# Attention with sorted key blocks, then a token mixer: turning q by head pairs laid side by side on GpSimd

## The chip, the cores and the metric

The kernel runs on one core of a Trainium2 chip. A core has five engines that run their own queues in order and wait for each other through semaphores: TensorE (PE in the profile: matmuls and transposes into PSUM), VectorE (DVE), ScalarE (ACT), GpSimd (POOL) and SyncE (SP, which here only issues transfers). The metric is the device time of one execution in microseconds. The kernel before takes 104.41 us (median of 3 runs, 104.3 to 104.9). The profile shows one execution; its span of 102.3 us leaves out some microseconds at the ends of the device time.

## What is computed

The reference, cut to what matters, with B = 4 batches, H = 8 heads, S = 768 tokens, D = 64, and 8 blocks of 96 tokens:

```python
P = sort_net                                   # (B, H, 8, 8), five rounds of row and column softmax
k_sorted = einsum('bhij,bhjcd->bhicd', P, k_blocks)
v_sorted = einsum('bhij,bhjcd->bhicd', P, v_blocks)
attn = softmax(q_block @ k_sorted_block.T / sqrt(D))      # inside each block of 96
x    = concat_heads(attn @ v_sorted_block)                # (B, S, 512)
W    = (x @ w_q) @ (x @ w_k).T / sqrt(64)                 # token mixer, (S, S) per batch
out  = relu(W @ x) @ w_out                                # (B, S, 512), float32
```

The inputs q, k and v are float32, each 1.5 MB a batch, and become bf16 as they are loaded.

## The kernel before

The kernel is written as a list of units. The text `ORDER` is that list: each item has a letter for its kind, the batch, a number, and at its end an engine (A, D, P or S) or, for TensorE units, a PSUM bank. A loop at the end of the kernel emits the items as they stand, so this order is the order on each engine's own queue; what one engine must wait for from another follows from the data. Nothing reorders at run time. A capital letter is TensorE work, and the small letter of the same name moves its result out of PSUM on ScalarE or VectorE.

For one batch the stages are these. `l` loads an input in the GpSimd queue (`l20P` is q of batch 2; the middle digit is the batch, the last 0 for q, 1 for k, 2 for v, 3 and 4 for weights). Tokens lie on partitions: token 6p + r is on partition p at position r. `n` builds the sorting matrices M from the 8x8 matrices, on GpSimd for batches 1 to 3. `Q` transposes q, `q` copies it to QT. `K` multiplies k by M, which sorts and transposes it, and `k` copies it to KT. `V` (or `F` and `A` for batch 0) sorts v; `R` moves the sorted rows between partitions by transfers of the SP queue. `S` and `e` give the scores and their exponentials, `P`, `r` and `x` the attention result, `T` and `t` its transpose. `J`, `W`, `G` and `H` are the token mixer, `d` copies a half of its query part to other partitions (on ScalarE, on VectorE, or by a transfer), `O`, `o` and `y` give and store the output. `Z` is fill: matmuls of zeros that keep TensorE running at the start, while the 8x8 softmax rounds (`c`) go on. `N` copies a single element on GpSimd out of a tile that is still being made: it holds the GpSimd queue, and so the loads behind it, back until that tile is there. The batches overlap: while batch 1 has its scores computed, batch 0 is in the mixer.

Around the change. A `Q` unit covers two of the six positions r and all four head pairs, so there are three units a batch. Each unit has 16 transposes (lines 244 to 250): one head at a time, 128 tokens by 64 dimensions as the stationary operand, the identity as the moving one with 128 columns. The two heads of a pair go to the lower and the upper half of the PSUM partitions. Its result fills one bank, which `q` copies out at once (line 252). The tiles Qn, Kn and Vn have three buffers each (lines 95 and 96), chosen by the batch modulo 3. The first half of q of batch 0 is loaded as float32 by SP into a borrowed tile, and ScalarE casts it into Qn (items `i04A`, `i05A`, lines 185 to 187); the second half comes by `l00P`.

The transposes, the copies out and all matmuls are recorded under the helper lines 140 (`mm`) and 144 or 146 (`copy`), so the profile's groups are told apart by the tiles.

Of the kernel before, what the change touches and what calls it, by code (L numbers as in the profile page):

```python
# [9 lines left out]
BF16 = mybir.dt.bfloat16  # L10
# [5 lines left out]


ORDER = """
l00P l01P l02P i00P i02P l03P c00D c01D i01D Z080 l11P c02D i03A Z250 c03D Z350 i04A l10P c04D Z440
i05A Q027 c05D Q016 q02A Q005 Z540 q00A b00D l12P B004 Z020 q01A n01D n00D l04P K010 u00A n03D K002  # L20
n11P n02D k01A K036 k00D K024 k03A S020 n10P k02D S012 e02A S056 F034 e01A S000 f03D l20P e05A F022
A035 f02A S066 a03D e00A A024 F012 e06A a02D F000 f01A K136 n21P f00D P044 A013 r04D A002 k13D a01A
n20P K100 x04D S036 k10A a00D K114 e03A S040 k11D P002 e04A P016 r00D Q115 x00D r01D P020 x01D q11A
Q104 r02D P032 q10A x02D V116 T005 v11A N11v l21P l30P r03D Q124 x03D V100 t00A V126 q12A v10D T015
T033 T022 v12A N11v N10v N12v l22P t03D S110 l32P t02D t01A S123 V136 e11A J012 v13D J005 e12A J032
S150 R12S j01D J025 R15S e15A S106 j00D R10S Q214 R11S d01D l31P Q203 e10A R14S q21D R13S W002 Q225
q20D d00A S160 w00D W014 q22A K126 w01D G003 e16A n30P k12A G013 K230 g01D K224 n31P k23A S136 k22D
H002 e13A K200 h00D S244 k20A H026 h02A S200 K212 e20A k21D O057 e24A H010 o05D S212 O046 h01A S234
e21A O007 e23A O033 o00D o04A P140 S264 o03A y02S Q302 r14D e26A x14D P116 S144 r11D Q313 x11D e14A
P100 q30A P134 r10D x10D V206 q31A O022 r13D x13D v20A V230 T103 v23A P126 T135 t10A r12D V210 x12D  # L30
O014 o02A v21A y01S V222 t13D T117 o01D v22A T126 V330 t11D y00S V304 t12D R20S S252 v30A Q327 R21S
v33D R25S J106 e25A R24S q32D R22S J115 R23S J126 V310 j10A J135 S222 v31D j11A W104 V326 e22A d11S
W115 w10D K300 v32D d10A G104 k30A K322 R30S K336 R32S w11A S300 k32A R33S k33D G114 R31S e30A R35S
K312 g11D R34S S366 k31D S354 e36A H110 e35A H106 h11D S312 h10A S334 P210 e33A O107 r21D e31A x21D
P204 O116 o10A r20D x20D P230 o11A P222 r23D H124 y10S x23D T207 h12A O126 r22D x22D t20A P300 O145
o12A r30D x30D T214 o14A T227 P242 t21D S325 t22A S340 r24D O134 x24D e32A T237 e34A o13D P312 J205
t23A y11S r31D P330 x31D J214 J225 P326 r33D j20A x33D J234 T303 d20S j21A W202 O155 t30A r32D d21S
w20D x32D W212 G203 w21A o15D P340 T312 r34D G213 y12S x34D T327 t31D g21A T336 t32D H220 t33A H202
H214 h22D J307 J316 h21D J327 O251 j30A d30A W300 h20D J336 O247 w30A j31A o25D G300 d31A o24A W316
O221 y22S w31D G310 o22A O237 g31A H320 o23A H312 H304 h32A O206 y21S O217 o20A O351 o21A h30D h31A  # L40
O340 y20S o35A O307 o34D y38S O321 y37S o30A O310 y33S o32D O337 o31A y35S y34S o33B y36S
"""


# [1 line left out]
def kernel(  # L46
# [11 lines left out]
    nc = tc.nc  # L58
    B, H, S, D = q.shape
# [3 lines left out]
    P = 128  # L63
    R6 = S // P
    SP = BLK // R6
    NP = H // 2
# [16 lines left out]
    sb = ctx.enter_context(tc.tile_pool(name="sb", bufs=1))  # L83
    psp = ctx.enter_context(tc.tile_pool(name="psp", bufs=1, space=bass.MemoryType.PSUM))

    def tiles(name, n, shape, dtype=BF16):
        return [sb.tile(shape, dtype, name=f"{name}{i}") for i in range(n)]

    PS = psp.tile([P, 8, 512], FP32, name="ps")
    ENG = {"A": nc.scalar, "D": nc.vector, "P": nc.gpsimd, "S": nc.sync}  # L90
# [2 lines left out]
    nc.sync.dma_start(out=Pm[:, 0:NB, :], in_=sort_net.rearrange("b h i j -> (b h) i j"))  # L93

    NIN = 3
    Qn, Kn, Vn = (tiles(n, NIN, [P, H, R6, D]) for n in ("Qn", "Kn", "Vn"))
    wqk = sb.tile([P, PT, 2, DH], BF16, name="wqk")
    wo = sb.tile([P, PT, DM], BF16, name="wo")

    def load(t, src, b):  # L100
        nc.gpsimd.dma_start(out=t[b % NIN].rearrange("p h r d -> p h (r d)"),  # L101
                            in_=src[b].rearrange("h (p r) d -> p h (r d)", p=P))

    QT = tiles("QT", 2, [P, NP, R6, P])
# [20 lines left out]
    idb = sb.tile([P, P], BF16, name="idb")  # L125
# [13 lines left out]
    def mm(o, w, x, start=True, stop=True, t=False):  # L139
        nc.tensor.matmul(o, w, x, is_transpose=t, start=start, stop=stop, skip_group_check=True)  # L140

    def copy(e, o, i):
        if e == "A":
            nc.scalar.copy(o, i)  # L144
        else:
            nc.vector.tensor_copy(o, i)  # L146

    def bf(n):
        return PS[:, n, :].bitcast(BF16)
# [3 lines left out]
    stage = mixT[0].rearrange("p a c r s -> p (a c r s)").bitcast(FP32).rearrange("p (h e) -> p h e", h=HQ)  # L153
# [21 lines left out]
    def u_i(b, n, e):  # L175
        if n == 0:
            nc.gpsimd.memset(idb, 0.0)
            nc.gpsimd.affine_select(out=idb, in_=idb, compare_op=ALU.not_equal, fill=1.0, base=0,
                                    pattern=[[-1, P]], channel_multiplier=1)
        elif n == 1:  # L180
            nc.vector.reduce_max(m_p, idb.rearrange("p (j s) -> p s j", s=SP), axis=AX.X)
        elif n == 3:
            nc.scalar.copy(Lx.rearrange("p i j s -> p (i j) s"),
                           idb[0:BH, 0:BH].unsqueeze(2).to_broadcast([BH, BH, SP]))
        elif n in (4, 5):
            h = 2 * n - 8
            copy(e, Qn[0][:, h:h + 2].rearrange("p h r d -> p h (r d)"), stage[:, h:h + 2])
        elif n == 2:
            for t in VT:
                nc.gpsimd.memset(t.rearrange("p i (h e) -> p i h e", e=DS)[:, :, :, D:DS], 1.0)  # L190
            for t in Vs:
                nc.gpsimd.memset(t[:, :, :, D:DS], 1.0)
            for t in KT:
                nc.gpsimd.memset(t[:, :, S:S + P - BLK], 0.0)
            for t in E:
                nc.gpsimd.memset(t[:, :, 2 * TH * BLK:EW], 0.0)
                nc.gpsimd.memset(t[:, NT - 1, 2 * (NB * NP - TH * (NT - 1)) * BLK:EW], 0.0)  # L197


    def u_l(b, n, e):  # L200
        if n == 3:
            for s, w in enumerate((moe_w_q, moe_w_k)):
                nc.gpsimd.dma_start(out=wqk[:, :, s, :], in_=w.rearrange("(t p) d -> p t d", p=P))  # L203
        elif n == 4:
            nc.gpsimd.dma_start(out=wo, in_=moe_w_out.rearrange("(t p) d -> p t d", p=P))
        elif b == 0 and n == 0:
            nc.gpsimd.dma_start(out=Qn[0][:, HQ:H].rearrange("p h r d -> p h (r d)"),  # L207
                                in_=q[0, HQ:H].rearrange("h (p r) d -> p h (r d)", p=P))
        else:
            load((Qn, Kn, Vn)[n], (q, k, v)[n], b)  # L210
# [30 lines left out]
            mm(PS[:, bank, :], filw[:, b, :], fil)  # L241


    def u_Q(b, n, bank):
        ps = bf(bank).rearrange("p (k r s) -> p k r s", k=NP, r=2)
        for r in range(2):
            for kp in range(NP):
                for hh in range(2):
                    mm(ps[hh * D:(hh + 1) * D, kp, r, :], Qn[b % NIN][:, 2 * kp + hh, 2 * n + r, :],
                       idb, t=True)  # L250

    def u_q(b, n, e, bank):
        copy(e, QT[b % 2][:, :, 2 * n:2 * n + 2, :].rearrange("p k r s -> p k (r s)"),
# [225 lines left out]
    for item in ORDER.split():  # L479
        kind, b, n, arg = item[0], int(item[1]), int(item[2:-1]), item[-1]  # L480
# [40 lines left out]
```

## Time and profile before

| what | before |
|---|---|
| device time, median of 3 | 104.41 us |
| span of the profiled execution | 102.3 us |
| granted TensorE clock | 1.00 on the mean |
| transposes of q | 192 in 12 units |
| GpSimd M for batches 1 to 3 | 6, 1.30 us each |
| loads issued by GpSimd | 15, 0.76 to 0.95 us of GpSimd each |
| QT copies | 9 on ScalarE at 1.02 us, 3 on VectorE at 0.68 us |

The page has one row for each group of instructions: line, engine, operation, result and operands, count, then busy time and mean duration, then the idle time of the engine just before. Durations of matmuls are latencies and overlap; the time that a unit takes is read from the start of its first matmul to the start of the next unit's. The part of the page in slices shows the rest: TensorE's row stands at 8 or 9 tenths from the start to the end, and the transfer row at 9 from the second slice to the 26th, some 2.5 to 66 us; after that transfers are few. GpSimd is busy in the first 40 us and idle afterwards.

```profile
PE   3999988889879998899999999789999999999940
POOL 5999667550018954000000000000000000000000
DMA  1899999999999999999999999641305150234992
```

### The profile page before, as it was taken

What the parts mean: (1) busy time and instruction counts of PE and PEld (TensorE: products, weight loads), DVE (VectorE), ACT (ScalarE), POOL (GpSimd) and SP (SyncE); (2) the same over time, 40 slices, a digit from 0 to 9 for tenths busy, and PEclk for the clock granted to TensorE, in tenths of its full rate; (3) what the DMA queues carried; (4) which work ended last, traced back from release to release, by engine and by line L of the source; (5) the groups of instructions that cost most, each with busy time, mean ns of one, the idle gap of its engine ahead of it and who ended that gap; (6) DMA issues with size and microseconds to landing.
All of it is one profiled execution on the core that took longest, in us unless ns stands there. A gap on an engine that the chain in (4) does not pass through costs nothing.

```text
span 102.3 us, 3324 instructions
## 1 busy us (share of the span) xinstructions
PE 91.3 (89%) x1411; PEld 59.3 (58%) x1420; DVE 71.2 (70%) x135; ACT 76.4 (75%) x115; POOL 24.6 (24%) x41
## 2 busy tenths in 40 slices
PE   3999988889879998899999999789999999999940
PEld 1234566678657686545867668556778665544410
DVE  3776787589987874653898966779979999304420
ACT  5254979949859997999699789995896446678430
POOL 5999667550018954000000000000000000000000
PEclk9999999999999999999999999999999999999999
DMA  1899999999999999999999999641305150234992
GB/s 17 280 212 205 202 193 199 203 208 201 204 208 204 207 200 247 254 217 204 209 297 205 317 352 202 172 132 77 135 0 210 40 205 0 87 136 195 372 345 103
DMA packets 19133, 19.57 MB, mean 191 GB/s; under 512 B 1904, under 2 KB 17200, under 8 KB 19120
## 3 DMA queue, kind: packets, MB, share of 16 engines
q0 software_dynamic: 13552, 9.70, 62.3%
q1 hardware_dynamic: 5568, 9.67, 28.1%
q8 instruction: 11, 0.18, 0.7%
q14 instruction: 2, 0.02, 0.0%
HBM read 20.19 MB, written 6.29 MB: 259 GB/s over the span
## 4 chain that ended last, share of the span: by engine, by line
PE 47%; DMA 30%; POOL 9%; ACT 7%; issue 2%; DVE 2%; ACTq 0%; DVEq 0%; POOLq 0%
PE ps L140 47%; DMA Vn<-in_v_dram 18%; DMA Kn<-in_k_dram 9%; DMA qD<-qkT 3%; POOL Kn L101 2%; ACT E L347 2%; ACT KT L144 1%; POOL wqk L203 1%; DVE mixT L453 1%; POOL E L197 1%; ACT qkT L144 1%; ACT mixT L451 1%; POOL Qn L207 1%; POOL Vn L101 1%; POOL Qn L101 1%
## 5 line engine op out<-in xcount | busy, mean ns | idle before, releaser
L347 ACT ACTIVATE E<-ps 96x960 bf16<-96x960 f32 (+1 forms) x28 | 24.0, 913 | 0.9 <-PE ps L140 0.9
L140 PE MATMUL ps<-wo,mixT 128*128 128x512 bf16 x88 | 22.5, 380 | 0.5
L381 DVE TENSOR_TENSOR X<-ps,R 96x896 bf16<-96x896 f32 (+1 forms) x20 | 20.1, 1006 | 0.6
L140 PEld LDWEIGHTS <-mixT 128*128 128x128 bf16 x96 | 8.5, 98 | 9.3 <-issue 0.8
L144 ACT COPY ot<-ps 128x512 f32<-128x512 f32 (+1 forms) x16 | 9.2, 581 | 5.2 <-PE ps L140 5.2
L140 PE MATMUL ps<-VT,E 96*128 96x65 bf16 x256 | 11.0, 193 | 0.7 <-DVE mixT L453 0.7
L140 PEld LDWEIGHTS <-E 96*128 96x128 bf16 x256 | 9.7, 97 | 2.9 <-issue 0.9
L140 PE MATMUL ps<-fil,filw 128*128 128x512 bf16 x27 | 9.3, 500 | 2.0 <-DVE filw L161 1.6
L453 DVE TENSOR_SCALAR mixT<-ps 128x1024 bf16<-128x1024 f32 x6 | 7.2, 1220 | 5.0 <-PE ps L140 4.9
L146 DVE COPY ot<-ps 128x512 f32<-128x512 f32 (+1 forms) x9 | 5.9, 658 | 6.0 <-PE ps L140 4.6
L140 PE MATMUL ps<-QT,KT 64*128 64x96 bf16 x256 | 9.8, 204 | 0.3 <-ACT KT L144 0.3
L144 ACT COPY QT<-ps 128x1024 bf16<-128x1024 bf16 x9 | 8.8, 1016 | 0.7 <-PE ps L140 0.6
L146 DVE CAST KT<-ps 128x768 bf16<-128x768 f32 x8 | 7.5, 948 | 2.5 <-PE ps L140 2.5
L231 POOL TENSOR_TENSOR M<-PTR,m_p 128x512 bf16<-128x512 bf16 x6 | 7.8, 1314 | 4.9 <-PE ps L140 3.1
L140 PEld LDWEIGHTS <-KT 64*128 64x128 bf16 x256 | 6.6, 94 | 3.9 <-issue 1.5
L140 PE MATMUL ps<-M,Kn 128*64 128x128 bf16 x192 | 7.6, 221 | 1.3 <-ACT XT L144 0.5
L140 PEld LDWEIGHTS <-Kn 128*64 128x64 bf16 x192 | 6.1, 109 | 3.1 <-DMA Kn<-in_k_dram 1.2
L140 PEld LDWEIGHTS <-X 96*128 96x128 bf16 x128 | 6.4, 98 | 1.6 <-issue 0.4
L140 PE MATMUL ps<-idb,X 96*128 96x96 bf16 x128 | 7.3, 206 | 0.0
L144 ACT CAST KT<-ps 128x768 bf16<-128x768 f32 x8 | 6.4, 799 | 0.9 <-PE ps L140 0.9
L140 PE MATMUL ps<-idb,Qn 128*64 128x128 bf16 x192 | 7.1, 221 | 0.0
L140 PEld LDWEIGHTS <-filw 128*128 128x128 bf16 x28 | 2.9, 118 | 7.1 <-issue 2.7
(77 smaller groups left out, 137.8 us busy)
## 6 DMA issues: line engine op xcount, KB each, us to landing
out_dram<-ot SPq DMA_DIRECT2D x9, 512.0 KB, 3.5
Kn<-in_k_dram POOLq DMA_DIRECT2D x4, 768.0 KB, 10.8
Vn<-in_v_dram POOLq DMA_DIRECT2D x4, 768.0 KB, 17.4
VT<-Vs SPq DMA_DIRECT2D x18, 132.0 KB, 4.4
Qn<-in_q_dram POOLq DMA_DIRECT2D x3, 768.0 KB, 15.5
out_dram<-ot SPq DMA_DIRECT2D x6, 256.0 KB, 2.1
mixT<-in_q_dram SPq DMA_DIRECT2D x1, 768.0 KB, 4.6
wo<-in_moe_w_out_dram POOLq DMA_DIRECT2D x1, 512.0 KB, 20.1
```

The lines of the kernel that those rows point to most:

```text
L101: nc.gpsimd.dma_start(out=t[b % NIN].rearrange("p h r d -> p h (r d)"), in_=src[b].rearrange("h (p r) d -> p h (r d)", p=P))
L140: nc.tensor.matmul(o, w, x, is_transpose=t, start=start, stop=stop, skip_group_check=True)
L144: nc.scalar.copy(o, i)
L146: nc.vector.tensor_copy(o, i)
L197: nc.gpsimd.memset(t[:, NT - 1, 2 * (NB * NP - TH * (NT - 1)) * BLK:EW], 0.0)
L203: nc.gpsimd.dma_start(out=wqk[:, :, s, :], in_=w.rearrange("(t p) d -> p t d", p=P))
L207: nc.gpsimd.dma_start(out=Qn[0][:, HQ:H].rearrange("p h r d -> p h (r d)"), in_=q[0, HQ:H].rearrange("h (p r) d -> p h (r d)", p=P))
L231: ENG[e].tensor_tensor(out=M[b % 2][:, h0:h1], in0=src.unsqueeze(2).to_broadcast([P, nh, SP, NB]), in1=m_p.unsqueeze(1).unsqueeze(3).to_br ...
L347: nc.scalar.activation(E[b % 2][:, n, 0:2 * w * BLK].rearrange("p (t a c) -> p a t c", a=2, c=BLK), PS[0:BLK, bank:bank + 2, 0:w * BLK].re ...
L381: nc.vector.tensor_mul(xo.rearrange("p (a t d) -> p a t d", a=2, d=D), avps(bank, w)[:, :, :, 0:D], rr[b, n][:, :, 0:w].unsqueeze(3).to_br ...
L451: nc.scalar.activation(o, i, ACT.Relu)
L453: nc.vector.tensor_relu(o, i)
```

## The change

[...] In the q tile the two heads of a pair are 384 elements apart[...]. The change adds a tile Qp in which, for each pair and position, the 64 dimensions of both heads stand side by side. New items `p` fill it on GpSimd, one copy for each head pair and batch (for batch 0 only for pairs 2 and 3; the casts `i04A` and `i05A` write the first two pairs straight into Qp). A Q unit then has 8 transposes of 128 columns in place of 16 of 64. Since q is copied out of Qn early, Qn keeps two buffers instead of three; Qp has one, so the copies of a batch come after the transposes of the batch before.

The order text is replaced as a whole. Its GpSimd part, which both tiles' waits hang on, reads before and after:

```text
before: l00 l01 l02 i00 i02 l03 l11 l10 l12 l04 n11 n10 l20 n21 n20 N11 l21 l30 N11 N10 N12 l22 l32 l31 n30 n31
after:  l00 l01 l02 i00 i02 l03 l11 p02 l10 p03 l12 l20 n10 n11 l04 n20 n21 p13 p11 p10 p12 N13 l21 p22 N13 N11 N12
        l32 l30 l22 p23 n31 p21 l31 p20 n30 p31 p33 p30 p32
```

And TensorE's order around the first V units of batch 1 and the Q units of batch 2:

```text
before: P016 Q115 P020 Q104 P032 V116 T005 Q124 V100 V126 T015 T033 T022 S110 S123 V136 J012 J005 J032 S150 J025 S106
        Q214 Q203 W002 Q225 S160 W014 K126 G003 G013 K230
after:  P046 K102 P020 T005 P032 Q124 V136 V110 Q115 T014 Q107 T026 T033 V120 J002 V103 J022 J017 S160 S125 W002 J037
        S133 S100 G002 W015 S146 S110 G012 S154 Q203 Q211 Q220 H002 H026 K224
```

At the start, the three Q units of batch 0 stand ahead of `Z5` and `B` in both. In the after order v of batch 3 is used before v of batch 2, the first transposes `T` of batch 0 come ahead of the first V unit, and of the 12 QT copies 6 instead of 3 are on VectorE.

The diff without the order text:

```diff
     NIN = 3
-    Qn, Kn, Vn = (tiles(n, NIN, [P, H, R6, D]) for n in ("Qn", "Kn", "Vn"))
+    Kn, Vn = (tiles(n, NIN, [P, H, R6, D]) for n in ("Kn", "Vn"))
+    Qn = tiles("Qn", 2, [P, H, R6, D])
+    Qp = sb.tile([P, NP, R6, 2, D], BF16, name="Qp")
...
     def load(t, src, b):
-        nc.gpsimd.dma_start(out=t[b % NIN].rearrange("p h r d -> p h (r d)"),
+        nc.gpsimd.dma_start(out=t[b % len(t)].rearrange("p h r d -> p h (r d)"),
...
         elif n in (4, 5):
             h = 2 * n - 8
-            copy(e, Qn[0][:, h:h + 2].rearrange("p h r d -> p h (r d)"), stage[:, h:h + 2])
+            copy(e, Qp[:, n - 4].rearrange("p r h d -> p h r d"),
+                 stage[:, h:h + 2].rearrange("p h (r d) -> p h r d", d=D))
...
+    def u_p(b, n, e):
+        ENG[e].tensor_copy(Qp[:, n].rearrange("p r h d -> p h r d"), Qn[b % 2][:, 2 * n:2 * n + 2])
+
     def u_Q(b, n, bank):
         ps = bf(bank).rearrange("p (k r s) -> p k r s", k=NP, r=2)
         for r in range(2):
             for kp in range(NP):
-                for hh in range(2):
-                    mm(ps[hh * D:(hh + 1) * D, kp, r, :], Qn[b % NIN][:, 2 * kp + hh, 2 * n + r, :],
-                       idb, t=True)
+                mm(ps[:, kp, r, :], Qp[:, kp, 2 * n + r].rearrange("p h d -> p (h d)"), idb, t=True)
```

More of the change, by code (lines that the diff above doesn't have):

```diff
@@ L18 @@
 ORDER = """
[L19 to L38, printed above, removed]
@@ L39 @@
-H214 h22D J307 J316 h21D J327 O251 j30A d30A W300 h20D J336 O247 w30A j31A o25D G300 d31A o24A W316
-O221 y22S w31D G310 o22A O237 g31A H320 o23A H312 H304 h32A O206 y21S O217 o20A O351 o21A h30D h31A
-O340 y20S o35A O307 o34D y38S O321 y37S o30A O310 y33S o32D O337 o31A y35S y34S o33B y36S
+l00P l01P l02P i00P i02P l03P c00D c01D i01D Z080 l11P c02D i03A Z250 c03D Z350 i04A p02P l10P p03P
+c04D Z440 i05A Q007 c05D Q016 q00A Q025 Z540 q02A b00D l12P B004 Z020 q01A n03D n02D K030 l20P u00A
+n00D K022 n01D n10P k03A K006 k02D K014 k00A S050 k01D n11P F032 e05A F016 F004 f03A f01D S020 f00A
@@ new lines @@
+S002 l04P A017 e00A A006 a01D S014 e02A F022 a00D A037 n20P f02D e01A S030 a03D K122 n21P e03A K134
+k12D A027 k13A K110 a02D P012 k11A P004 r01D S066 x01D S040 e06A p13P e04A P046 r00D K102 x00D p11P
+P020 k10A r04D p10P x04D T005 p12P r02D P032 x02D t00A Q124 V136 r03D q12D V110 v13A N13v l21P Q115
+x03D T014 v11A Q107 t01A T026 T033 t02D V120 q10A t03D J002 p22P v12D N13v N11v N12v l32P l30P l22P
+q11A V103 J022 J017 v10D p23P j00A S160 S125 d00S W002 e16A n31P J037 R15S e12A S133 w00D R14S j01D
@@ new lines @@
+S100 G002 R10S e10A R11S d01D p21P W015 R12S S146 R13S w01D e13A S110 l31P p20P G012 e11A S154 n30P
+Q203 g01A Q211 e14A q20D Q220 q21D H002 e15A H026 q22D h02A K224 h00D K200 k22A O057 k20A K232 o05A
+K214 k23D S200 k21A H016 h01D S262 e20A S234 e23A S240 O017 e24A S214 o01D O026 e26A e21A V300 o02D
+P132 v30A V314 r13D P126 x13D v31A S250 e25A P114 r12D x12D P102 O001 p31P r11D r10D S226 x11D O030
+p33P e22A x10D T115 p30P o03A P146 T124 t11A o00D y01S T100 p32P V332 t12D y00S O041 v33A r14D t10D
@@ new lines @@
+V224 x14D o04A J110 v22D T137 y02S V212 t13A J101 v21D V234 J121 J130 v23A V206 j10D Q303 j11A d10D
+W101 Q312 v20A d11D w10D W110 K324 q31D q30A R24S K316 R20S w11D G101 k32D R23S k31A K332 R25S G111
+R21S k33A K304 R22S V326 g11A k30D Q320 v32A H102 q32D H124 h10A H116 R34S h12D S360 R31S R33S e36A
+S312 R35S h11D S340 R32S e31A O155 R30S e34A S332 P236 e33A O114 r23D x23D o15A P220 o11A O123 r22D
+x22D P214 o12A O132 r21D x21D T223 o13A P200 t22A P246 y11S S354 r20D r24D O102 x20D e35A T213 x24D
@@ new lines @@
+o10A T205 P340 t21D y10S S326 t20A r34D T232 x34D e32A P333 J205 r33D t23A S300 x33D P326 e30A J225
+J212 r32D x32D j20A P313 P300 d20A J232 r31D W205 r30D T337 j21A x31D T326 w20A d21S W212 t33A G205
+x30D w21A T313 t32A G215 t31D T302 g21A O143 t30A H220 o14A H214 H206 h22A J302 h21D y12S J313 h20A
+J322 O241 j30D J333 d30A W300 O222 o24A j31D w30D d31A W313 G307 o22A w31D O256 G317 o25A O235 g31D
+y22S H320 o23A H312 H306 h32D O214 y21S O205 o21A O351 o20A h30D h31A O340 y20S o35A O307 o34D y38S
@@ L42 @@
+O321 y37S o30D O310 y33S o32A O337 o31A y35S y34S o33B y36S
 """
```

## The prediction

> **What bounds the kernel now.** I read the page from the top: first the busy shares, then the shares of the chain of work that ended last.
>
> ```profile
> PE 91.3 (89%) x1411; PEld 59.3 (58%) x1420; DVE 71.2 (70%) x135; ACT 76.4 (75%) x115; POOL 24.6 (24%) x41
> ...
> PE 47%; DMA 30%; POOL 9%; ACT 7%; issue 2%; DVE 2%; ACTq 0%; DVEq 0%; POOLq 0%
> ```
>
> TensorE is busy 89%, but the chain gives it only 47%: 30% is input transfers. Then the chain in order of time, which says where each rules.
>
> ```profile
> 10.32 18.44 DMA Vn<-in_v_dram
> ...
> 30.44 8.81 DMA Kn<-in_k_dram
> ...
> 43.69 8.45 PE ps L140 x135
> ```
>
> Until 28.8 us the clock is set by the arrival of v of batch 1 (v1), then by k of batch 2 (k2) at 39.25. From 43.7 on it is TensorE almost without a break. So TensorE work saved after about 40 us counts; before that a delay hides only up to what TensorE waits for v1 (1.1 us, view of waits) and k2 (0.2).
>
> What does a Q unit cost? The timeline of TensorE, and two rows by shape:
>
> ```profile
> 48.88 0.61 PE L140 MATMUL ps<-VT,E 96*128 96x65 bf16 x14
> 49.42 0.39 PE L140 MATMUL ps<-QT,KT 64*128 64x96 bf16 x10
> 49.74 0.64 PE L140 MATMUL ps<-idb,Qn 128*64 128x128 bf16 x16
> 50.31 1.17 PE L140 MATMUL ps<-VT,E 96*128 96x65 bf16 x28
> ...
> 76.51 0.65 PE L140 MATMUL ps<-XT,wqk 128*128 128x384 bf16 x3
> 77.00 0.60 PE L140 MATMUL ps<-VT,E 96*128 96x65 bf16 x14
> 77.43 0.81 PE L140 MATMUL ps<-XT,wqk 128*128 128x384 bf16 x4
> ```
>
> Take start to start, not durations, which overlap. A Q unit of 16 half-width transposes takes 50.31 - 49.74 = 0.57 us. The single records show why it isn't twice a full-width one: the halves of a pair start 2 to 4 ns apart, and pairs follow at 56 ns, exactly the pitch of the full-width 128-column transposes of qkT. So 8 x 56 = 0.45 us is streaming and 0.12 is something else. The same 14 P matmuls take 77.43 - 77.00 = 0.43 us between full-width J units and 49.42 - 48.88 = 0.54 before S, which uses half the rows. Passing between shapes thus costs about 0.1 us: 0.10 leaving full width, 0.12 leaving half columns (K, F, G, old Q), 0.14 leaving half rows (S, H; 10 matmuls take 0.32 before another shape, 0.18 before their own).
>
> Last, GpSimd, which the change loads:
>
> ```profile
> 30.20 0.18 POOL L333 COPY gate<-Vs 1x1 bf16<-1x1 bf16 x1 [8.46 <-ACT Vs L144]
> 30.44 0.94 POOL L101 DMA_DIRECT2D Kn<-in_k_dram  x1
> 31.37 0.88 POOL L101 DMA_DIRECT2D Qn<-in_q_dram  x1
> 32.24 0.65 POOL L333 COPY gate<-Vs 1x1 bf16<-1x1 bf16 x3
> 33.05 1.75 POOL L101 DMA_DIRECT2D Vn<-in_v_dram  x2 [0.17 <-issue]
> 34.78 0.89 POOL L101 DMA_DIRECT2D Kn<-in_k_dram  x1
> 35.67 1.38 POOL L231 TENSOR_TENSOR M<-PTR,m_p 128x512 bf16<-128x512 bf16 x1
> ```
>
> It is idle 76% of the span, yet here it works strictly in line: each load that it issues holds it 0.9 us.
>
> [...] The fill matmuls (Z) show the two states as pitches of 427 and 216 ns at the start.
>
> **The change part by part.**
>
> *Half-width to full-width transposes.* 192 become 96, but the streaming is the same, 12 x 0.45 us. Gained are shape switches only. Counting both orders with the new shapes from the first V unit of batch 1 to the end: before 54 switches (21 out of full width at 0.100, 15 out of half columns at 0.122, 18 out of half rows at 0.136) = 6.4 us; after 45 (20, 9 and 16) = 5.3. The units, at their unswitched pitches (O 0.86, P 0.44, Q 0.45, T 0.34, V 0.32, J 0.49 and 0.16, W 0.22, K 0.34, G 0.44, S 0.18, H 0.22), sum to 58.8 and 58.6. Total 65.2 against 63.9: **1.3 us saved** on TensorE.
>
> *Fourteen copies p on GpSimd*, 768 elements per partition each. No row shows one. Lower bound: memsets of 224 and 608 elements take 0.28 and 0.60 us, so 0.83 ns an element and 0.1 fixed: 0.73 us[...]. [...] (The M row, 1.3 us for 512, has two inputs.) I take 1.0.
>
> *The start.* Before, Q0 begins at 9.63. After, its last copy p03 stands behind l03 (ends 8.6), l11, p02 and l10: 8.6 + 0.9 + 1.0 + 0.9 + 1.0 = 12.4. B now waits behind Q0 and Z5: K begins at 12.4 + 1.35 (Q) + 0.1 + 0.86 (Z) + 0.2 (B) + 0.86 (B to K as before) = 15.8 instead of 12.96. Then 11.2 us of units and switches and 2.8 of small waits to Q124: 29.8 (the waits as before: 12.96 to 28.80 is 15.8, less 1.3 at v1, less 11.7 by the same ledger). Its copies p1x need q1, which lands at 9.45 + 15.5 = 24.95, and end at about 29.0. V136 follows at 30.25; v1 is there since 28.75. This loses 1.4 us against 28.80. The casts i04 and i05 now write strided; they end by 9.4, behind p03's 12.4, and cost nothing.
>
> *Q2, the step that decides.* All Q2 units need p20, the last of four copies, since every unit runs over all pairs. GpSimd's line there is p22, three gates, l32, l30, l22, p23, n31, p21, l31, p20. Its head p22 needs q2. Input transfers run back to back in issue order; before, v1 landed at 28.75, wo at 31.3, q2 at 16.31 + 18.8 = 35.1, so a q takes 3.8. After, q2 is issued ahead of wo: 28.75 + 3.8 = 32.55. The line behind it: gates 0.8 (32.24 to 33.05 above), four loads 3.6, M 1.3, four copies 4.0 = 9.7. So Q203 starts at **42.25**. TensorE gets there at 30.25 + 8.1 (units and switches) + 0.6 (waits as before) = 38.95: a stall of 3.3 us. The order puts H0 and K2 behind Q203, so nothing fills it, and k2, landed at 39.25, stops being the limit.
>
> *Later parts.* k3 is issued behind p21, at about 40.3 instead of 34.8; it landed at 58.6 because four loads were ahead of it, and they still are: no cost. p3x waits for q3 (about 50) and is over by 54; Q303 comes near 60: no cost. Two q buffers: q3 overwrites q1, whose copies are done by 29: no cost. More Q evictions on VectorE (0.68 us for ScalarE's 1.02) are off the path.
>
> *The sum.* From Q203 the after order has 51.6 of units and 36 switches, 4.2: 55.8. The before order from K230 (39.29) to the end of its last O unit (97.9) took 58.6 where its ledger says 55.5: 3.1 of small waits, which I carry over. 42.25 + 55.8 + 3.1 + 4.4 (97.9 to the end of the span, 102.3) + 2.1 (104.41 less 102.3) = **107.6 us**.
>
> **The rivals.** (1) *The copies keep up.* GpSimd's idle 76% speaks for it; its line of loads speaks against. Then the ledger alone counts: 104.41 - 1.3 = 103.1. (2) *The stall is paid back.* Copies of 0.73 start Q203 at 41.2, and the evictions, caught up during the stall, leave 1.0 of waits instead of 3.1: 41.2 + 55.8 + 1.0 + 6.5 = 104.5. For it: some waits are for ScalarE and VectorE; against: they have no store of work to do ahead. (3) *Worse.* [...]: 43.25 + 1.7 + 55.8 + 3.1 + 6.5 = 110.4. [...]
>
> **How the numbers follow.** Forecast 0.62, rival 1 0.12, rival 2 0.10, rival 3 0.16. The copy bounds alone move the forecast to 106.6 and 108.6, the waits by another 1. The range 104.5 to 110.0 leaves out rival 1 and the far end of rival 3. Faster by over 0.5%: 0.12; within: 0.06 (over half of rival 2); slower: 0.82.
>
> **What would show it.** In the profile after: 96 transposes of Q at 56 ns in units of 0.45 us; 14 GpSimd copies of 0.7 to 1.3 us; the first Q unit near 12.4; q2 landing near 32.5; the wait of TensorE for Qp at Q203 as the longest after the start, 2 to 5 us, with the GpSimd loads and copies on the chain ahead of it; after it, TensorE nearly unbroken. If p20 ends before TensorE arrives, the forecast is wrong; if a copy takes under 0.4 us it fails in size.

## The result and the profile after

The kernel after takes 108.72 us (median of 5 runs) against 104.41 before: ratio 1.041, interval 1.037 to 1.045. The prediction was 107.6 us, slower. Executions of the kernel after come in two groups, near 108.6 and near 110.4 us; the profile shown here is of the second, which differs at the start, as told below, and the times compared are of the first.

The busy shares, the granted clock in 40 slices, and the shares of the chain that ended last, from the page of the kernel after:

```profile
PE 92.3 (85%) x1315; PEld 61.1 (56%) x1324; DVE 71.2 (66%) x136; ACT 76.4 (70%) x115; POOL 35.6 (33%) x55
...
PEclk9999669999999998559999999999999999999997
...
PE 61%; POOL 17%; ACT 7%; DVE 7%; issue 5%; ACTq 0%; POOLq 0%; DVEq 0%
```

There are 96 matmul instructions fewer, yet TensorE is busy for 1 us longer. Input transfers have left the chain (30% before) and GpSimd has come in (9% to 17%). The clock row has two dips, which the row of the kernel before hasn't:

```profile
PEclk9999999999999999999999999999999999999999
```

The chain of the kernel after, in order of time, says where GpSimd stands in it:

```profile
36.26 0.88 POOL Vn L104
...
38.90 0.83 POOL Qp L249
39.73 1.25 POOL M L235
40.98 0.76 POOL Qp L249
41.74 0.88 POOL Kn L104
42.62 0.85 POOL Qp L249
...
43.51 3.73 PE ps L143 x29
```

Three loads (two of them left out here), a copy, an M, a copy, a load and the last copy, p20, stand one behind the other without a gap; TensorE starts when the last of them ends. TensorE's own timeline around the Q units of batch 1 and of batch 2 (start, length, group, and in brackets the idle time before it):

```profile
30.40 0.60 PE L143 MATMUL ps<-VT,E 96*128 96x65 bf16 x14
30.83 0.61 PE L143 MATMUL ps<-idb,Qp 128*128 128x128 bf16 x8
31.28 0.81 PE L143 MATMUL ps<-Vn,M 128*128 128x384 bf16 x4
...
43.51 2.74 PE L143 MATMUL ps<-idb,Qp 128*128 128x128 bf16 x24 [3.75 <-POOL Qp L249]
46.19 0.60 PE L143 MATMUL ps<-qkT,Ab 64*128 64x512 bf16 x1
```

A Q unit between full-width neighbours takes 31.28 - 30.83 = 0.45 us, and P ahead of it 0.43: no switch is paid there. Batch 2 waits 3.75 us for the copies. Its three units then take 46.19 - 43.51 = 2.68 us, not 1.35: the single records show a pitch (the time from one start to the next) of 107 ns where batch 1 has 56, and the granted clock is 0.50 from 42.53 to 49.35 us. The same pitch of 107 ns stands in Q0 at the start, after a wait of 1.4 us for p03 (granted clock 0.50 from 11.81 to 15.22 us).

### The profile page after: what moved, and what is told of

Same layout as the page of the kernel before. It is cut to its first block, busy times and chain, and to the rows that moved or that the text cites. A ratio compares the mean times of both kernels' runs of the same rounds, so it can differ in the third digit from the quotient of the medians.

```text
span 108.6 us, 3151 instructions
## 1 busy us (share of the span) xinstructions
PE 92.3 (85%) x1315; PEld 61.1 (56%) x1324; DVE 71.2 (66%) x136; ACT 76.4 (70%) x115; POOL 35.6 (33%) x55
## 4 chain that ended last, share of the span: by engine, by line
PE 61%; POOL 17%; ACT 7%; DVE 7%; issue 5%; ACTq 0%; POOLq 0%; DVEq 0%
PE ps L143 61%; POOL Qp L249 4%; POOL Kn L104 2%; POOL Vn L104 2%; ACT Vs L147 2%; ACT mixT L456 2%; POOL Qn L104 2%; DVE XT L149 1%; POOL wqk L207 1%; DVE X L386 1%; DVE VT L149 1%; POOL M L235 1%; DVE M L235 1%; POOL E L201 1%; ACT E L352 1%
## 5 line engine op out<-in xcount | busy, mean ns | idle before, releaser
L147 ACT COPY ot<-ps 128x512 f32<-128x512 f32 (+1 forms) x19 | 10.8, 577 | 6.9 <-PE ps L143 6.7
L143 PE MATMUL ps<-idb,Qp 128*128 128x128 bf16 x96 | 9.3, 263 | 5.4 <-POOL Qp L249 5.4
L249 POOL COPY Qp<-Qn 128x768 bf16<-128x768 bf16 x14 | 11.4, 836 | 7.7 <-DMA Qn<-in_q_dram 7.7
L143 PEld LDWEIGHTS <-Qp 128*128 128x128 bf16 x96 | 8.0, 121 | 6.4 <-POOL Qp L249 5.8
L458 DVE TENSOR_SCALAR mixT<-ps 128x1024 bf16<-128x1024 f32 x7 | 8.5, 1222 | 3.5 <-ACT ot L147 1.9
L147 ACT COPY XT<-ps 128x768 bf16<-128x768 bf16 x10 | 8.0, 804 | 1.8 <-PE ps L143 1.6
L456 ACT ACTIVATE mixT<-ps 128x1024 bf16<-128x1024 f32 x5 | 5.0, 1027 | 5.5 <-PE ps L143 5.5
L147 ACT CAST KT<-ps 128x768 bf16<-128x768 f32 x10 | 7.9, 801 | 1.1 <-PE ps L143 0.8
L149 DVE COPY QT<-ps 128x1024 bf16<-128x1024 bf16 x6 | 4.1, 691 | 6.2 <-PE ps L143 6.1
L147 ACT COPY QT<-ps 128x1024 bf16<-128x1024 bf16 x6 | 5.9, 1030 | 2.7 <-PE ps L143 2.7
```

The lines of the kernel that those rows point to most:

```text
L249: ENG[e].tensor_copy(Qp[:, n].rearrange("p r h d -> p h r d"), Qn[b % 2][:, 2 * n:2 * n + 2])
L456: nc.scalar.activation(o, i, ACT.Relu)
L458: nc.vector.tensor_relu(o, i)
```

## The experiments

The theory: the change saves some switches between shapes on TensorE, and loses more because the copies p2x stand in GpSimd's queue among loads that hold it 0.9 us each. Its rivals: the new order is slow by itself; the later start is the cost; the copies themselves are.

**1. The order without the copies** (e1). All `p` items are dropped, the tiles and the transposes are those of the kernel before.

```diff
-    Kn, Vn = (tiles(n, NIN, [P, H, R6, D]) for n in ("Kn", "Vn"))
-    Qn = tiles("Qn", 2, [P, H, R6, D])
+    Qn, Kn, Vn = (tiles(n, NIN, [P, H, R6, D]) for n in ("Qn", "Kn", "Vn"))
...
-                mm(ps[:, kp, r, :], Qp[:, kp, 2 * n + r].rearrange("p h d -> p (h d)"), idb, t=True)
+                for hh in range(2):
+                    mm(ps[hh * D:(hh + 1) * D, kp, r, :], Qn[b % NIN][:, 2 * kp + hh, 2 * n + r, :],
+                       idb, t=True)
```

> The after order without the fourteen copies p and with the half-width transposes straight from Qn (three q buffers): the order alone. Theory (the copies' line on GpSimd is the cost): Q0 starts near 9.6 us again, K near 13, V136 at about 28.9 when v1 lands, no stall at Q203, clock at full speed throughout; 28.9 + 64.9 (units and switches of this order with the old transposes) + 3.9 (small waits as before) + 6.5 (tail and ends) = 104.2 us. Rival (the new order itself is slow, whatever the copies): 107 us or more.

Measured: 106.02 us (105.20 to 106.91), ratio 1.014, 1.006 to 1.021, between theory and rival. V136 starts at 28.70 as expected and most of the loss is gone, but 1.8 us more are left than expected. TensorE's unit G012 waits 1.8 us for `wk` of VectorE. VectorE and GpSimd in e1, from their timelines:

```profile
35.51 2.69 DVE L145 COPY qD<-qkT 64x384 bf16<-64x384 bf16 x1
38.23 0.29 DVE L145 COPY wk<-ps 96x256 bf16<-96x256 bf16 x1
```

```profile
35.00 0.88 POOL L100 DMA_DIRECT2D Qn<-in_q_dram  x1
35.87 0.89 POOL L100 DMA_DIRECT2D Vn<-in_v_dram  x1
36.76 1.33 POOL L230 TENSOR_TENSOR M<-PTR,m_p 128x512 bf16<-128x512 bf16 x1
38.00 0.94 POOL L100 DMA_DIRECT2D Kn<-in_k_dram  x1
```

The copy `d01`, which takes 0.25 us in the kernel before, takes 2.69: it reads and writes SBUF, and it ends (38.20) 0.11 us after GpSimd's M. Experiment 7 follows this up.

**2. The kernel after without p20 to p23** (e2).

```diff
-J002 p22P v12D ... p23P ... p21P ... p20P
+J002 v12D ...
```

> The kernel after without the four copies p20 to p23; batch 2 is then computed with the q of batch 1, which Qp still holds. Theory: Q203 starts when TensorE arrives, near 39.8 us instead of 43.5, no half clock behind it; 39.8 + 55.8 + 3.1 + 6.5 = 105.2 us, so 3.4 us less than the kernel after, and what stays above the kernel before is the later start. Rival (k2 or the loads behind take over as the limit): 107 to 108.5 us, with K224 waiting for Kn.

Measured: 107.17 us (106.82 to 107.65), ratio 1.029: a miss, only 1.5 of the 3.4 us. The profile shows no wait for GpSimd at Q203 any more, but the same copy `d01` at 2.69 us (36.10 to 38.79; M of GpSimd ends at 38.67), G012 waiting 1.8 us behind it, and half clock after that. The run took one wait away and let another in; it doesn't measure the first.

**3. The copies ahead of the loads** (e3). Every copy is made; p23, p21 and p20 move up to p22.

```diff
-p22P ... N13v N11v N12v l32P l30P l22P p23P n31P p21P l31P p20P n30P
+p22P p23P p21P p20P ... N13v N11v N12v l32P l30P l22P n31P l31P n30P
```

> The kernel after with only GpSimd's queue changed: p23, p21, p20 directly behind p22, ahead of the gates, the three loads, n31 and l31, so every copy is still made. Theory (what counts is the loads in the line, not the copies): p20 ends near 37.1 us, ahead of TensorE at 39.8, no stall; 105.2 us as without the copies. Rival (the transfers issued 3 us later then leave the transfer engines idle and v3 or q3 become the limit): a new wait at V300 near 50 us and 106.5 to 108 us.

Measured: 105.49 us (median of 12, 104.07 to 108.10); the ratio, 1.005 (1.001 to 1.008), is that of the seven executions up to 105.62, whose mean is 104.8. The profile, of an execution at 104.07, has the four copies in one train, Q203 at 38.17, and full clock throughout:

```profile
32.68 3.13 POOL L248 COPY Qp<-Qn 128x768 bf16<-128x768 bf16 x4 [0.35 <-DMA Qn<-in_q_dram]
```

So the copies themselves are not the cost: with the same work, but p20 done at 35.8 instead of 43.5, those seven executions take 3.9 us less than the kernel after. No new wait at V300 shows. The times spread more than those of any other kernel. In the five executions above 106 us the mean granted clock is 0.963 to 0.984, which is 3.4 to 7.7 us at half clock (an estimate: the share missing to 1, times two, of their spans of 104.2 to 106.3 us), in the others 0.993 to 1.000; none of the five has a profile, so what TensorE waited for is open.

**4. Fill in the waits** (e4). The waits stay; TensorE multiplies zeros meanwhile.

```diff
-i04A p02P l10P p03P c04D Z440 i05A Q007
+i04A p02P l10P p03P c04D Z4100 i05A Q007
...
-S154 n30P Q203
+S154 n30P Z5123 Q203
```

> The kernel after with fill matmuls of zeros while TensorE has nothing to do: 10 instead of 4 in the last fill ahead of Q0, and 12 (2.6 us) ahead of Q203. The stall for the copies stays. Theory (the half clock behind a stall costs about 1 us at Q0 and 2.6 us at Q203 to K2): pitches of 56 ns in all Q units, 216 in O, Q203 still at about 43 us; 42.8 + 55.8 + 3.1 + 6.5 = 108.2 less what the earlier K gives nothing for: 105.5 to 106.5 us. Rival (the half clock is hidden, since evictions set the pace then): 108 to 108.7 us.

Measured: 106.93 us (106.90 to 107.06), ratio 1.025: 1.8 us less than the kernel after, 0.4 above the expected range, and far from the rival. The three units of Q2 in its TensorE timeline, still waiting for the copies:

```profile
42.12 1.51 PE L142 MATMUL ps<-idb,Qp 128*128 128x128 bf16 x24 [1.34 <-POOL Qp L248]
```

Full clock again: 1.00 granted from 39.38 to 42.80 us, with TensorE busy for 2.08 us of them, and 0.995 on the mean of the execution. From Q203 (42.12) to V300 (51.73) it takes 9.6 us, in the profile of the kernel after 11.6. So 1.8 of the 4.3 us are not the waits, which stay in e4, but the clock behind them.

**5. The shape alone** (e5). The kernel before with full-width transposes; all batches use the q that the two casts lay side by side, heads 0 to 3 of batch 0, and q has two buffers, as in the kernel after.

```diff
-                for hh in range(2):
-                    mm(ps[hh * D:(hh + 1) * D, kp, r, :], Qn[b % NIN][:, 2 * kp + hh, 2 * n + r, :],
-                       idb, t=True)
+                mm(ps[:, kp, r, :], Qp[:, kp % 2, 2 * n + r].rearrange("p h d -> p (h d)"), idb, t=True)
```

> The kernel before with full-width transposes and nothing else of the change: no copies p, the old order. Every Q unit transposes the two head pairs that the two ScalarE casts put side by side (batch 0, heads 0 to 3), so all batches use that q; the loads of q still run. It measures what the transposes themselves bring. Theory (only the switches between shapes are saved, the streaming is the same): Q units of 0.45 us, 0.47 us less before K230, which k2 at 39.25 swallows, and 0.37 less after it: 104.0 us, 0.4 below the kernel before. Rival (half as many transposes take half the time, 12 x 0.28 = 3.4 us in all, 0.9 of it behind K230): 103.4 us or less.

Measured: 104.20 us (21 runs), ratio 0.998, 0.997 to 0.9995. The pitch of the transposes is 56 ns, a unit takes 48.72 - 48.26 = 0.46 us. So the time of streaming is not halved, as the pairs in the trace of the kernel before had said, with 2 to 4 ns between their halves and 56 from pair to pair. The gain of 0.2 us is smaller still than the expected 0.4. K230 starts at 39.24 after a wait of 0.56 us, hardly ahead of 39.29 before: k2 lands at 30.32 + 8.9 = 39.22, and the M that it is multiplied by is done at 39.20.

**6. The old start** (e6). The kernel after, with batch 0 as before: no p02 and p03.

```diff
-                mm(ps[:, kp, r, :], Qp[:, kp, 2 * n + r].rearrange("p h d -> p (h d)"), idb, t=True)
+                if b > 0:
+                    mm(ps[:, kp, r, :], Qp[:, kp, 2 * n + r].rearrange("p h d -> p (h d)"), idb, t=True)
+                    continue
+                for hh in range(2):
+                    mm(ps[hh * D:(hh + 1) * D, kp, r, :], Qn[0][:, 2 * kp + hh, 2 * n + r, :], idb, t=True)
```

> The kernel after, but batch 0 as in the kernel before: casts into Qn, half-width transposes from Qn, no p02 and p03. Theory: Q0 begins near 9.7 us instead of 12, K near 13.0, V136 at about 28.9 instead of 30 to 31.3; the line of GpSimd for batch 2 then starts with q2 at 32.7 and ends near 41.5 to 42.3, so Q203 gains only about 1 to 2 us and the stall there grows: 106.5 to 107.5 us. Rival (the start is what costs): 104.5 to 105.5 us.

Measured: 108.48 us (108.40 to 108.52), ratio 1.039: 0.2 us gained, less than expected. K starts at 13.04 and V136 at 28.69, as early as the V units before the change; but Q203 starts at 41.42, when p20 is done. From the view of waits (total, times, longest):

```profile
PE ps L142 <- POOL Qp L247: 4.9, 3, 4.2
```

The start can be bought back, but the stall grows from 3.7 to 4.2 us and half clock follows it again (0.50 granted from 39.18 to 46.00), so little of the gain is left.

**7. The order, with one copy on ScalarE** (e7). As e1, with `d01D` made `d01A`.

> The order alone, as in the run with the half-width transposes and no copies, with one copy of the mixer's query part (qD, batch 0, second half) moved from VectorE to ScalarE. In that run the copy took 2.69 us on VectorE, SBUF to SBUF, while GpSimd issued three loads and made M in one train, against 0.25 us elsewhere. Theory [...]: G012 no longer waits 1.9 us for wk, Q203 near 37.8 us, no half clock: 103.3 to 104.0 us. Rival (VectorE was waiting for data[...]): the same 105.2 to 106.9 us.

Measured: 104.12 us (22 runs), ratio 0.9975, 0.996 to 0.999: by the two ratios about 1.7 us less than e1, by one letter. In the profiles, with 1.000 granted in e7 and 0.995 in e1, Q203 starts at 38.35 instead of 39.45. GpSimd's line is the same as in e1. The copy wasn't waiting for data in e1: its operand `qkT` is done at 35.48 and the copy starts at 35.51. In e1 and e2 it stood through the rest of a load, another load and an M of GpSimd, and it ends 0.11 and 0.12 us after that M. In the kernel after it came among the same loads and took 0.49 us, ending at 38.13, 0.12 us after the load under way; in e3, where GpSimd made only gates at that time (35.74 to 36.41), it took 0.25. What holds the copy up, and why it stood longer in e1 and e2, isn't shown.

**8. Rearranged** (e8). As e6, and GpSimd's queue written anew: k2 and v3 issued ahead of p1x; q3, v2 and k3 behind it, all before q2 lands; then the four copies in one train; n31 and n30 behind a gate on the first QT copy of batch 2.

```diff
-l04 n20 n21 p13 p11 p10 p12 N13 l21 p22 N13 N11 N12 l32 l30 l22 p23 n31 p21 l31 p20 n30 p31 p33 p30 p32
+l04 l21 n20 n21 l32 p13 p11 p10 p12 l30 l22 l31 p22 p23 p21 p20 N20q n31 n30 p31 p33 p30 p32
```

> The change rearranged: batch 0 with half-width transposes straight from Qn; GpSimd issues k2 and v3 ahead of the copies p1x, and q3, v2 and k3 right behind them, before q2 lands; p22, p23, p21, p20 then follow one after the other from 32.7 us; n31 and n30 wait (one gate) until the first QT copy of batch 2. The copies for batches 1 to 3 stay. Theory: V136 at 28.9, p20 done at 36, no stall at Q203 (37.3), K224 when k2 lands at 39.3; from there 7.6 to V300 and 48.4 to the last O unit as in the run with the copies first, and 6.8 to the end: 102.1 us, up to 103. Rival (something else takes the place of the stall, [...] or k2): 104 us or more.

Measured: **103.01 us** (102.98 to 103.25), ratio 0.987, 0.985 to 0.989: faster than the kernel before and the kernel after, at the upper end of the expectation. GpSimd, then TensorE at Q2:

```profile
30.14 0.89 POOL L103 DMA_DIRECT2D Kn<-in_k_dram  x1
32.62 3.13 POOL L247 COPY Qp<-Qn 128x768 bf16<-128x768 bf16 x4 [1.58 <-DMA Qn<-in_q_dram]
```

```profile
36.82 0.39 PE L142 MATMUL ps<-QT,KT 64*128 64x96 bf16 x10
37.13 1.58 PE L142 MATMUL ps<-idb,Qp 128*128 128x128 bf16 x24
```

The loads are out of the way when q2 lands, the last copy ends at 35.75, and TensorE comes at 37.13 and doesn't wait for it.

**9. Rearranged, with half-width transposes and no copies** (e9). As e8, with the tiles and transposes of the kernel before.

> The rearranged version without the copies p and with half-width transposes straight from Qn in all batches (three q buffers), all else in the same order: what the full-width transposes bring where their copies are hidden. Theory (switches only): 0.5 us of switches ahead of K224, part of it swallowed by k2, and 0.57 behind it: 103.0 + 0.6 to 1.0 = 103.6 to 104.0 us. Rival (the copies cost what the transposes gain): 103.0 us or less.

Measured: 103.48 us (103.38 to 103.62), ratio 0.991, 0.989 to 0.992, a little under the expected range. So in this arrangement the full width brings 0.5 us by the times, 0.4 by the ratios, and the order with the earlier loads 1.0 (e7, the order without them, has 0.3). Q203 starts at 37.62 and K224 at 40.23, in e8 at 37.13 and 39.70. But from K224 to the last O unit both take about the same (56.2 us here, 56.1 in e8), where the ledger, the prediction's sum of units and switches, gives e8 0.57 less. O057 in e8:

```profile
41.27 1.04 PE L142 MATMUL ps<-wo,mixT 128*128 128x512 bf16 x3 [0.71 <-ACT mixT L458]
```

In e9 it starts at 41.28, after a wait of 0.18 us. So the 0.5 us that e8 is ahead at K224 are lost here, and what it gains comes later.

**10. The kernel after once more** (e10), unchanged.

> The kernel after once more, unchanged, for a second profile beside the others. Theory: Q203 near 42 to 43.5 us, set by the end of p20; half clock behind it; 108.6 us.

Measured: 108.69 us, ratio 1.041, 1.038 to 1.043. Its profile, of an execution at 110.49 us, again has Q203 at 43.56 and half clock at Q0 and behind Q203 (0.948 granted on the mean).

## Why the prediction was right, by its own steps

*Streaming.* Right: pairs had run together already (2 to 4 ns apart), 0.45 us a unit and 56 ns a transpose in the profile after, and 0.2 us in all from the shape alone (e5).

*The switches, 1.3 us.* Right in kind. The arrangement of e8 gains 1.4 us in all, but not as the ledger splits it: 0.4 to 0.5 come with the full width (e9), where the ledger has 1.0 for it; the rest of that went into the wait ahead of O057.

*The copies.* Predicted 1.0 us; measured 0.78 from start to start (3.13 for four), near the lower bound of 0.73, which the memsets of the kernel before gave. The upper bound, behind the 108.6 us that the prediction gives for slow copies, was shown by no trace.

*The start.* Predicted: Q0 at 12.4, K at 15.8, V136 at 30.25. p03 ends at 11.97 and the rest of Q0 starts at 12.0. K starts at 15.03 and V136 at 29.75 in e2 and e3, which have the same start at full clock. In the profile after, K is at 16.6 and V136 at 31.3, because Q0 and the fill behind it run at half clock (pitch 107 ns in Q0, 427 in the fill).

*q2 and GpSimd's line.* q2 was to land at 32.55 and landed at 12.74 + 20.0 = 32.74. p20 was to be done at 42.25; it was at 43.46 in the profile after, where the later v13 also held the first gate and v12 held the last for 0.7 us, and at 42.06 in e4. That 42.06 comes so near is in part luck: p22 starts at 33.31 there, 0.8 later than worked out, and the four copies take 0.8 less than the 4.0 put down for them. The stall was 3.7 us, predicted 3.3. It is the cause: e3 has the same copies without it.

*The remainder.* Predicted from Q203 to the last O unit 55.8 + 3.1 = 58.9 us. The 97.9 that this was worked out with is the start of the last matmul, not the end of its unit; what is missing stands in the 4.4 behind it, so the sum isn't touched. Taken to the same matmul, it is 100.86 - 42.12 = 58.74 in e4, at full clock, and 104.19 - 43.51 = 60.68 in the profile after.

*What failed: the clock.* That the wait would halve it stood only in rival 3, with a chance of 0.16 and 1.7 us for it, beside slower copies (Q203 at 43.25), which didn't come. No trace had shown either of the two. As for the clock, in the kernel before the fill matmuls follow at 427 ns up to the first rise of the clock at 7.25 us and at 216 after it, the granted clock is 1.00 from there to 102.8, and the longest wait of TensorE after the start is 1.1 us. The half clock came, and costs 1.8 (e4). Without it the same waits give 106.9 us; the forecast of 107.6 lies between, 1.1 too small for the kernel as it is and about 0.6 too large for one with full clock (e4's profiled execution, 107.06). That excess isn't the copies', which the later q2 makes up for, but small terms: 0.1 up to Q203, 0.2 to the last matmul, 0.3 behind it. So two errors that partly cancel brought the number near: the direction and the stall were understood, the nearness is in part luck. The forecast didn't count the clock at all, and no run had yet shown what a stall like its own, of 3.3 us, does to it.

*The rivals.* Rival 1 fails for this queue. For e8 its number comes out, 103.01 measured and 103.1 worked out, but split otherwise and with loads issued earlier, so this is in part luck. Rival 2 fails: the stall was not paid back. Stepping through the runs, the loss of 4.3 us splits into half clock 1.8 (after to e4), stall 2.1 (e4 to the 104.8 of e3), start and earlier loads 1.8 (e3 to e8), less the 1.4 by which e8 beats the kernel before. These are differences along one path and add up by construction. In the profiled executions of e4 and e3 (107.06 and 104.07, the lowest of its twelve) the stall is 3.0 and the start 1.1, so the border between these two is not sharp. e6 shows that the start alone brings 0.2 while the stall stands.

The clock can be read more closely. In the clock records of these traces it changes only in steps of 3.41 us, counted from its first rise (in the kernel after, at steps 2, 3, 11, 13 and 30), and that rise comes at different times (4.98 us in the profile after, 5.54 in e2, 7.25 in the profile before, 7.45 in e3). So the record divides the run into stretches, and here how busy TensorE was in one goes with the clock of the next. Busy times in such stretches, of the kernel after, then of e2 (the first column after the length is TensorE's; the number behind the five engines is the clock, 1.00 or 0.50):

```profile
8.39:11.80 3.41, 1.38 (x7) 0.60 (x7) 2.53 (x10) 1.41 (x5) 3.41 (x5) 1.00 1.31 203
...
39.11:42.53 3.42, 0.65 (x18) 0.31 (x12) 0.00 (x0) 3.05 (x5) 3.42 (x4) 1.00 1.17 191
42.53:45.94 3.41, 2.43 (x24) 2.44 (x24) 1.13 (x2) 0.00 (x0) 2.19 (x3) 0.50 1.22 243
45.94:49.35 3.41, 3.31 (x34) 1.86 (x34) 2.12 (x3) 1.72 (x3) 0.00 (x0) 0.50 1.27 230
```

```profile
8.95:12.37 3.42, 1.74 (x14) 0.97 (x15) 2.80 (x10) 1.08 (x4) 3.42 (x5) 1.00 1.31 203
36.26:39.67 3.41, 1.60 (x36) 1.09 (x32) 2.81 (x2) 2.37 (x3) 3.39 (x5) 1.00 1.19 163
```

In the kernel after, the stretch with 1.38 us of matmuls is followed by half clock (11.80 to 15.22, which is Q0), and the one with 0.65 by two at half: the 2.43 us of the first of these don't bring the clock back, the 3.31 of the second do. In e2 the start, with the same wait of 1.4 us for p03, falls otherwise into the stretches, 1.74 us lie in this one, and the clock stays; the one with 1.60 at the wait for `d01` is followed by a fall. In all stretches of the profiles before and after, from the first rise to the last matmul, and in those read of e1, e2, e3, e4, e6, e8 and e10, each at full clock with 1.60 us or less was followed by a fall but one: the last matmuls of e6 fill 1.56 us (100.62 to 104.03), and the record stays at full. Each at full clock with 1.74 us or more kept it. So the border near 1.6 isn't sharp, and the busy time may not be all that counts. Stretches at half clock also show in the mean granted clock of an execution: one of them in 107 us takes 0.016 off it (an estimate: half of 3.41 us). It is 0.947 in the profile after, which has three and a little at the end, and 0.959 to 0.968 in the three executions near 108.6 us, which would be one fewer (an estimate). That theirs spare Q0 is likely, but none of them has a profile.

## What to carry to other kernels

Before two half-width operations are joined, look at the start times: if they start together, as here (2 to 4 ns apart), the join can bring as little as here, 0.2 us in all (e5). An engine that is idle for most of the span can still be the limit where its queue is worked in line: count what stands ahead of the item that someone waits for, loads that it issues included (0.9 us of GpSimd each here), and put the awaited work first. A stall on TensorE costs more than its length when the clock falls behind it (1.8 us here); in e4, with fill matmuls in the wait, it stayed (0.995 to 1.000 granted).

## What the runs showed of the hardware that I had not expected

While GpSimd issued loads back to back and then made an M, a VectorE copy from SBUF to SBUF took 2.69 us instead of 0.25 (e1, e2); one letter, the same copy on ScalarE at 0.51 us, took about 1.7 us off the kernel (e7). In the stretches of 3.41 us that were read, TensorE's clock fell for the next one when it had been busy for 1.60 us or less, with the one exception at the end of e6, and stood at 1.74 or more. So a wait of 1.4 us cost the clock in the kernel after, where it left 1.38 us of work in its stretch, and not in e2, where it left 1.74.
